# Attention, expert layer and FFN in one kernel: a conversion operation moved between an activation's maximum and its low part, two first products side by side at each group boundary, and two weight pieces converted around expert 7's third block

## The chip, the cores and the metric

The kernel runs on one core of one Trainium2 chip. The metric is the device time of one execution in microseconds (us). The engines are named as the profile names them: PE is TensorE (matmuls), PEld its weight loads, DVE is VectorE, ACT is ScalarE, POOL is GpSimd and SP is SyncE, whose queue issues most of the loads.

## The reference

Three stages follow each other; float64 weights `w_in` and `w_out` come in for the last one.

```python
def reference(**kw):
    attn_out = _attn_ref(...)                    # windowed attention with memory slots
    x = attn_out.transpose(0, 2, 1, 3).reshape(1536, 512)
    x = _moe_ref(x, w_gate, w1, w2, capacity)    # top-1 of 8 experts, 512 -> 1024 -> 512, at most 384 rows each
    return _moe2_ref(x, w_in, w_out)

def _moe2_ref(x, w_in, w_out):                   # 1536 x 512 -> 2048 -> 512
    h = x @ w_in
    g = np.maximum(0.01 * h, h)
    return (g @ w_out).astype(np.float32)
```

## The kernel before

**Precision.** Every large product is made of three matmuls: each operand is split into a high part (rounded to the matmul's format) and a low part (the rest), and high x low, high x high and low x high are summed in PSUM. The high part is a cast on ACT, the low part a subtraction on DVE.

**Experts.** `expert(e)` runs the eight experts one after the other. A branch at L762 (`self.tc.If(cnt > j * P)`) executes `block` for the third 128 rows where an expert has that many; expert 7 has. `block` transposes the gathered rows into `tp` (L858), makes `xc` (high: ACT L860, low: DVE L861), does 12 matmuls for each of two halves of the hidden layer (L874), takes the maximum in two halves of the columns (ACT L877, DVE L878 into `hh`), transposes `hh` (L883), splits it (`ht`, ACT L885 and DVE L886) and does the second product (L892). Then come the first 256 rows in six phases: `units` (L772) and `rows` (L779), whose relu parts are `hs` (ACT L824, DVE L825). In expert 7 the phases also transpose the first 1024 gathered rows of the FFN's input (`make_x`: PE L699 into the one `tp` buffer or an `acc` buffer, high ACT L701, low DVE L702).

**Pieces.** The FFN's weights are 32 float64 pieces of 128 x 512, in four quarters of eight (four of `w_in`, kind A, and four of `w_out`, kind B). A piece is loaded by SP (five `raw` buffers) and made into a float32 by bit operations in `wide_stages`: two ACT operations (L132, L133), then six DVE operations (L135, L137, L139, L141, L142, L143), then the split: ACT L121 (high) and DVE L122 (low). `feed(n)` advances this by n steps. One step issues, in this order, the split of the piece before last, the six DVE operations of the last piece, and the two ACT operations of a new one. `FEED[7]` gives expert 7 four steps, `FEED_FFN` names the units of a quarter that are followed by a step.

**FFN.** 1536 sorted rows are three groups `g` of 512; each of the four quarters `q` of the hidden layer has four column blocks `f`. A unit (q, g, f) has a first product `gemm3` (12 matmuls, L945), then `act_h`, then a second product `gemm4` (12 matmuls, L965), which runs two units behind. `act_h` is a chain that changes engine at every step:

```python
nc.scalar.copy(out=t, in_=hp)                                   # ACT L951
nc.vector.scalar_tensor_tensor(out=t, in0=hp, scalar=0.01, in1=t, op0=ALU.mult, op1=ALU.max)   # DVE L952, the maximum
nc.scalar.copy(out=gt[:, 0, :], in_=t)                          # ACT L953, high
nc.vector.tensor_tensor(out=gt[:, 1, :], in0=t, in1=gt[:, 0, :].bitcast(F32), op=ALU.subtract)  # DVE L954, low
```

The second products of a group accumulate in four PSUM tiles `acc`, of which there are four in all. `add_up` scales them and adds them into `total` and `rest` (ACT L977 in the first quarter, DVE L979 after it); the next group's first `gemm4` needs the same four tiles. In the last quarter POOL stores each finished tile (L981). Instructions of an engine run in the order in which the code issues them; waits between engines are semaphores set by the tiles' dependencies.

Of the kernel before, what the change touches and what calls it, by code (L numbers as in the profile page):

```python
# [25 lines left out]
E, F1, F2 = 8, 1024, 2048  # L26
# [6 lines left out]
NQ = 4  # L33
# [9 lines left out]
        (2, 0, 0, 3, 2, 1), (2, 0, 0, 3, 2, 1), (2, 0, 0, 1, 1, 0), (1, 1, 1, 1, 0, 0))  # L43
AHEAD = ((0, (0, 1)), (0, (2, 3)), (None, ()), (1, (0, 1)), (1, (2,)), (1, (3,)))
RETIRE = (None, ("A", 0), None, ("A", 1), ("B", 0), ("B", 1))
FEED_FFN = (0, 2, 3, 4, 6, 7, 8, 10, 11)
# [7 lines left out]
class Builder:  # L54
# [69 lines left out]
    def wide_stages(self, raw, dst, eng):  # L124
# [11 lines left out]
                                op0=ALU.is_ge, op1=ALU.mult)  # L136
        dv.tensor_scalar(out=c[1], in0=c[0], scalar1=3, scalar2=0x3FFFFFFF,  # L137
# [55 lines left out]
    def weights_gen(self):  # L193
        flying, count = [], 0

        def advance():
            for rec in list(flying):
                rec[1] += 1
                if rec[1] == 1 or rec[1] == rec[2]:
                    next(rec[0], None)  # L200
                    if rec[1] > 1:
                        flying.remove(rec)
                        self.ready.add(rec[3])

        for kind, e, i, m in self.items:
# [7 lines left out]
            if e == E:  # L213
                advance()
                st = self.wide_stages(raw, (dst[:, 0, m, :], dst[:, 1, m, :]),
                                      self.nc.vector)
                next(st)
                flying.append([st, 0, self.flight, (kind, e, i, m)])
                yield
                continue  # L220
# [14 lines left out]
        while flying:  # L235
            advance()
            yield

# [286 lines left out]
    def prologue(self):  # L525
        nc = self.nc
        with ExitStack() as ctx:
# [48 lines left out]
            NU = 2 * NI  # L576
            self.W, self.ready, self.raws, self.items = {}, set(), [], self.weight_items()
# [173 lines left out]
    def expert(self, e):  # L751
# [7 lines left out]
        if nj > 2:  # L759
            cnt, nat = self.cnts.pop(e), self.natx.pop(e, [])  # L760
            for j in range(2, nj):
                with self.tc.If(cnt > j * P):  # L762
                    self.block(e, j, nat[j - 2] if j - 2 < len(nat) else None)
# [87 lines left out]
    def block(self, e, j, nat):  # L851
        nc = self.nc
        if nat is None:
            nat = self.gather(self.tab, e * self.nj + j, self.xs)
# [6 lines left out]
        nc.vector.tensor_tensor(out=xc[:, 1], in0=tp, in1=xc[:, 0].bitcast(F32), op=ALU.subtract)  # L861
        y = self.mps.tile([P, DM], F32, name="acc", tag="acc", bufs=4)
# [62 lines left out]
    def ffn(self):  # L925
# [21 lines left out]
        def act_h(s):  # L947
            hp = hps.pop(s)
            t = self.mp.tile([P, GT], F32, name="t", tag="o", bufs=2)
            gt = gs[s] = self.mp.tile([P, 2, GT], F32R, name="gt", tag="hg", bufs=4)  # L950
            nc.scalar.copy(out=t, in_=hp)  # L951
            nc.vector.scalar_tensor_tensor(out=t, in0=hp, scalar=0.01, in1=t, op0=ALU.mult, op1=ALU.max)  # L952
            nc.scalar.copy(out=gt[:, 0, :], in_=t)  # L953
            nc.vector.tensor_tensor(out=gt[:, 1, :], in0=t, in1=gt[:, 0, :].bitcast(F32), op=ALU.subtract)  # L954
# [29 lines left out]
        steps = [(q, g, f) for q in range(NQ) for g in range(NG) for f in range(HQ)]  # L984
        for n, s in enumerate(steps):
            q, g, f = s
            gemm3(s)
            act_h(s)
            if 1 < n < len(steps) - 2:
                gemm4([steps[n - 2]])  # L990
            if q == 0 and g == 1:
                self.make_x(2, f, nat)
            self.quarter = q + 1
            self.feed(n % len(steps[::NQ]) in FEED_FFN)
        gemm4(steps[-4:-3])
        gemm4(steps[-3:-2])
        gemm4(steps[-2:])
# [61 lines left out]
```

## Time and profile before

Three timed executions took 596.17, 596.9 and 598.88 us; the median is 596.9. The profiled execution took 594.74 us.

| of the profiled execution | us | share of the span |
|---|---|---|
| its own time | 594.74 | |
| span, first to last instruction | 593.0 | |
| PE busy with matmuls | 533.7 | 90% |
| PE weight loads | 432.0 | 73% |
| DVE busy | 402.5 | 68% |
| ACT busy | 298.6 | 50% |
| POOL busy | 119.6 | 20% |

The span runs from the first to the last instruction; 1.7 us of the execution lie outside it. The shares are averages over attention (to about 110 us), routing and experts (to about 307 us) and the FFN (from there to the end), which have different limits. Matmuls are pipelined: a group of 12 shows a busy time a little longer than the distance from its start to the next group's.

### The profile page before, as it was taken

To read this page: it belongs to the slowest core of one execution; us is meant where nothing else is said; L and a number is where in the kernel's file an instruction comes from. 1 tells how busy PE (TensorE), PEld (TensorE's weight loads), DVE (VectorE), ACT (ScalarE), POOL (GpSimd) and SP (SyncE) were. 2 spreads that over 40 slices of the span, in tenths; PEclk is the share of its full clock that TensorE was granted. 3 is DMA by queue.
4 is the path that set the end of the run, shared out by engine and by line. 5 is a ranking of instruction groups with operands and counts; after the bars stand their busy time and mean duration, and the time that the engine had idled before them with its cause. 6 is when DMAs were issued, how large, how long until landed. Compare 5 with 4: busy or idle time off the path is not lost.

```text
span 593.0 us, 9379 instructions
## 1 busy us (share of the span) xinstructions
PE 533.7 (90%) x3338; PEld 432.0 (73%) x3338; DVE 402.5 (68%) x680; ACT 298.6 (50%) x520; POOL 119.6 (20%) x144
## 2 busy tenths in 40 slices
PE   7799957997997997899998999998999999999995
PEld 5566635795986975677976878877878788778884
DVE  5776776877175357672787877868888788882442
ACT  7999735846173357861544464543443444422220
POOL 7333235028320015633202000000000000000222
PEclk8999976999997999899999999999999999999999
DMA  8998959998769439975343212212113111000111
GB/s 194 199 200 197 243 192 278 389 329 195 162 202 332 135 103 329 329 230 161 108 131 120 75 68 71 72 55 88 49 59 83 35 60 37 0 1 0 72 71 71
DMA packets 66378, 84.85 MB, mean 143 GB/s; under 512 B 23168, under 2 KB 39568, under 8 KB 66320
## 3 DMA queue, kind: packets, MB, share of 16 engines
q1 hardware_dynamic: 60016, 66.46, 38.5%
q0 software_dynamic: 5296, 15.77, 8.8%
q10 hardware_dynamic: 1008, 1.84, 0.8%
q8 instruction: 38, 0.62, 0.4%
q14 instruction: 20, 0.16, 0.1%
HBM read 70.66 MB, written 13.39 MB: 142 GB/s over the span
## 4 chain that ended last, share of the span: by engine, by line
DVE 30%; PE 11%; issue 8%; ACT 7%; POOL 2%; DMA 1%; POOLq 0%; ACTq 0%; DVEq 0%
DVE t L952 4%; PE acc L965 4%; DVE gt L954 4%; ACT gt L953 4%; DVE c L139 3%; DVE c L142 3%; DVE c L135 3%; DVE ring L122 3%; PE h L945 3%; DVE c L141 2%; DVE c L137 2%; DVE total L979 2%; POOL out_dram L981 2%; DVE c L143 1%; ACT ring L225 1%
## 5 line engine op out<-in xcount | busy, mean ns | idle before, releaser
L965 PE MATMUL acc<-ring,gt 128*128 128x512 f32 x576 | 140.7, 394 | 11.0 <-DVE total L979 4.3
L945 PE MATMUL h<-x,ring 128*128 128x512 f32 x576 | 138.8, 390 | 1.1 <-ACT x L701 1.1
L965 PEld LDWEIGHTS acc<-ring,gt 128*128 128x128 f32 x576 | 108.5, 190 | 37.4 <-ACT t L951 6.8
L945 PEld LDWEIGHTS h<-x,ring 128*128 128x128 f32 x576 | 107.7, 188 | 23.7 <-ACT x L701 1.5
L953 ACT CAST gt<-t 128x512 fp32r<-128x512 f32 x48 | 29.8, 621 | 110.4 <-DVE t L952 110.4
L981 POOL DMA_INDIRECT out_dram<-total,srt x8 | 8.3, 1039 | 249.3 <-DVE total L979 248.1
L954 DVE TENSOR_TENSOR gt<-t,gt 128x512 fp32r<-128x512 f32 x48 | 33.3, 694 | 33.0 <-ACT gt L953 33.0
L951 ACT COPY t<-h 128x512 f32<-128x512 f32 x48 | 28.1, 585 | 49.8 <-PE h L945 45.7
L952 DVE SCALAR_TENSOR_TENSOR t<-h,t 128x512 f32<-128x512 f32 x48 | 32.9, 684 | 30.0 <-ACT t L951 30.0
L772 PE MATMUL h<-xsT,ring 128*128 128x256 f32 x384 | 48.8, 284 | 0.7 <-DVE ring L229 0.7
L825 DVE SCALAR_TENSOR_TENSOR hs<-h,hs 128x512 fp32r<-128x512 f32 x32 | 21.7, 687 | 39.9 <-ACT hs L824 39.9
L772 PEld LDWEIGHTS h<-xsT,ring 128*128 128x128 f32 x384 | 47.1, 191 | 1.4 <-ACT ring L225 1.1
L779 PE MATMUL acc<-ring,hs 128*128 128x512 f32 x192 | 45.6, 391 | 0.0
L229 DVE TENSOR_TENSOR ring<-raw,ring 128x1024 fp32r<-128x1024 f32 x37 | 43.2, 1219 | 2.4 <-ACT ring L225 1.9
L225 ACT CAST ring<-raw 128x1024 fp32r<-128x1024 f32 x43 | 42.6, 1057 | 0.7 <-DMA raw<-in_moe_w_dram 0.7
L779 PEld LDWEIGHTS acc<-ring,hs 128*128 128x128 f32 x192 | 35.3, 188 | 7.0
L640 POOL DMA_INDIRECT nat<-xs,tab x24 | 27.5, 1145 | 54.2 <-PE tp L735 32.8
L824 ACT ACTIVATE hs<-h 128x512 fp32r<-128x512 f32 x32 | 18.9, 606 | 24.9 <-PE acc L779 23.9
L874 PE MATMUL h<-ring,xc 128*128 128x512 f32 x72 | 21.1, 446 | 8.7 <-ACT xc L860 7.8
L229 DVE TENSOR_TENSOR ring<-more,ring 128x1024 fp32r<-128x1024 f32 x21 | 24.6, 1222 | 0.8 <-ACT ring L225 0.5
L874 PEld LDWEIGHTS h<-ring,xc 128*128 128x128 f32 x72 | 14.9, 215 | 13.1 <-ACT xc L860 8.5
L784 PE MATMUL h<-ring,xsT 128*128 128x512 f32 x72 | 21.7, 458 | 3.1 <-DMA nat<-xs,tab 1.5
(184 smaller groups left out, 823.0 us busy)
## 6 DMA issues: line engine op xcount, KB each, us to landing
raw<-in_moe_w_dram SPq DMA_DIRECT2D x43, 512.0 KB, 7.0
more<-in_moe_w_dram SPq DMA_DIRECT2D x21, 512.0 KB, 7.0
raw<-in_moe_w_in_dram SPq DMA_DIRECT2D x16, 512.0 KB, 4.1
raw<-in_moe_w_out_dram SPq DMA_DIRECT2D x16, 512.0 KB, 3.3
kn<-in_k_dram SPq DMA_DIRECT2D x16, 192.0 KB, 2.8
qn<-in_q_dram SPq DMA_DIRECT2D x16, 192.0 KB, 4.6
xs<-x POOLq DMA_DIRECT2D x16, 192.0 KB, 4.6
ys<-o SPq DMA_DIRECT2D x12, 256.0 KB, 9.3
```

The lines of the kernel that those rows point to most:

```text
L225: self.nc.scalar.copy(out=hi, in_=raw)
L229: eng.tensor_tensor(out=lo[:, j:j + n], in0=raw[:, j:j + n], in1=hi[:, j:j + n].bitcast(F32), op=ALU.subtract)
L640: self.nc.gpsimd.indirect_dma_start(out=t, out_offset=None, in_=src, in_offset=bass.IndirectOffsetOnAxis(ap=idx[:, col:col + 1], axis=0))
L772: nc.tensor.matmul(hps[f // 2][:, f % 2 * 256:f % 2 * 256 + 256], w["A", f // 4][:, wi, k, c], xs[xi][:, k, :], start=(n == 0), stop=(n == ...
L779: nc.tensor.matmul(y[j], hs[f // 2][:, hi, c:c + P], w["B", f // 4][:, wi, f % 4, :], start=(f == 0 and n == 0), stop=(f == 7 and n == 2))
L874: nc.tensor.matmul(hp[i], xc[:, xi, k, :], w[:, wi, k, :], start=(n == 0), stop=(n == 11))
L945: nc.tensor.matmul(hps[s], w[:, wi, k, c], X[g][:, xi, k, :], start=(n == 0), stop=(n == 11))
L951: nc.scalar.copy(out=t, in_=hp)
L952: nc.vector.scalar_tensor_tensor(out=t, in0=hp, scalar=0.01, in1=t, op0=ALU.mult, op1=ALU.max)
L953: nc.scalar.copy(out=gt[:, 0, :], in_=t)
L954: nc.vector.tensor_tensor(out=gt[:, 1, :], in0=t, in1=gt[:, 0, :].bitcast(F32), op=ALU.subtract)
L965: nc.tensor.matmul(acc[g][i], gt[s][:, hi, i * P:(i + 1) * P], ws[s][:, wi, s[2], :], start=(s[2] == 0 and n == 0), stop=(s[2] == HQ - 1 a ...
```

## The change

`wide_stages` yields once more, so that the first of the six DVE operations (L135 before, L136 now) can be issued alone. The new `between`, called in `act_h` ahead of the low part, issues that operation for a piece whose two ACT operations have been issued; the next step then issues only the other five. The FFN's loop goes by groups, and at a boundary the last second product of a group comes ahead of the next group's second first product. `FEED_FFN` has eight units instead of nine. In expert 7 `block_x` (the transposes and `xc`) is taken out of the branch, one conversion step follows it ahead of the branch, and one follows the block; expert 7 thus has six steps instead of four.

```diff
+BLOCK_FEED = 1
-FEED_FFN = (0, 2, 3, 4, 6, 7, 8, 10, 11)
+FEED_FFN = (1, 2, 3, 5, 7, 9, 10, 11)
@@ wide_stages
         dv.scalar_tensor_tensor(out=cf[0], in0=cf[0], scalar=MIN_HIGH * MIN_HIGH, in1=hi_f,
                                 op0=ALU.is_ge, op1=ALU.mult)
+        yield
         dv.tensor_scalar(out=c[1], in0=c[0], scalar1=3, scalar2=0x3FFFFFFF,
@@ weights_gen
                 rec[1] += 1
+                if rec[1] == 1 and not rec[4]:
+                    next(rec[0])
                 if rec[1] == 1 or rec[1] == rec[2]:
@@
+    def between(self):
+        for rec in self.flying:
+            if rec[1] == 0 and not rec[4]:
+                next(rec[0])
+                rec[4] = True
+                return
@@ expert
             for j in range(2, nj):
+                xc = None
+                if e == E - 1 and j == 2:
+                    xc = self.block_x(nat[0])
+                    self.feed(BLOCK_FEED)
                 with self.tc.If(cnt > j * P):
-                    self.block(e, j, nat[j - 2] if j - 2 < len(nat) else None)
+                    self.block(e, j, nat[j - 2] if j - 2 < len(nat) else None, xc)
+            if e == E - 1:
+                self.feed(BLOCK_FEED)
@@ act_h
             nc.scalar.copy(out=gt[:, 0, :], in_=t)
+            self.between()
             nc.vector.tensor_tensor(out=gt[:, 1, :], in0=t, in1=gt[:, 0, :].bitcast(F32), op=ALU.subtract)
@@ ffn
-            if 1 < n < len(steps) - 2:
-                gemm4([steps[n - 2]])
...
+                if f == 0 and n:
+                    gemm4(groups[n - 1][2:3])
+                    gemm4(groups[n - 1][3:])
+                if f > 1 and n + 1 < len(groups):
+                    gemm4(steps[f - 2:f - 1])
```

**DVE in the FFN, a unit with a conversion step.** Before, in the order of the program, the maximum and the low part of a unit stand together and the step's seven operations follow:

```order
L952 SCALAR_TENSOR_TENSOR t<-h,t 128x512
L954 TENSOR_TENSOR gt<-t,gt 128x512
L122 TENSOR_TENSOR ring<-c,ring 128x512
L135 SCALAR_TENSOR_TENSOR c<-c,raw 128x512
L137 TENSOR_SCALAR c<-c 128x512
L139 SCALAR_TENSOR_TENSOR c<-c 128x512
L141 TENSOR_SCALAR c<-c 128x512
L142 TENSOR_TENSOR c<-raw,c 128x512
L143 TENSOR_TENSOR c<-c 128x512
```

Now, at the same place (L974 is the maximum and L977 the low part; L136 was L135, and L139 to L145 were L137 to L143):

```order
L974 SCALAR_TENSOR_TENSOR t<-h,t 128x512
L136 SCALAR_TENSOR_TENSOR c<-c,raw 128x512
L977 TENSOR_TENSOR gt<-t,gt 128x512
L123 TENSOR_TENSOR ring<-c,ring 128x512
L139 TENSOR_SCALAR c<-c 128x512
L141 SCALAR_TENSOR_TENSOR c<-c 128x512
L143 TENSOR_SCALAR c<-c 128x512
L144 TENSOR_TENSOR c<-raw,c 128x512
L145 TENSOR_TENSOR c<-c 128x512
```

One operation has moved from the step to the place between maximum and low part; the count is the same.

**PE at a group boundary of the FFN** (from the second quarter's first group, `x_4887`, to its second, `x_5117`). Before, first and second products alternate:

```order
L945 MATMUL h<-x_4887,ring 128x512 x12
L965 MATMUL acc<-ring,gt 128x512 x12
L945 MATMUL h<-x_5117,ring 128x512 x12
L965 MATMUL acc<-ring,gt 128x512 x12
L945 MATMUL h<-x_5117,ring 128x512 x12
L965 MATMUL acc<-ring,gt 128x512 x12
L945 MATMUL h<-x_5117,ring 128x512 x12
L965 MATMUL acc<-ring,gt 128x512 x12
```

Now (L967 is the first product, L988 the second, `x_4913` and `x_5143` the same two groups):

```order
L967 MATMUL h<-x_4913,ring 128x512 x12
L988 MATMUL acc<-ring,gt 128x512 x12
L967 MATMUL h<-x_5143,ring 128x512 x12
L988 MATMUL acc<-ring,gt 128x512 x24
L967 MATMUL h<-x_5143,ring 128x512 x24
L988 MATMUL acc<-ring,gt 128x512 x12
```

The two last second products of the old group stand together, and two first products of the new group stand between them and its first second product, where there was one.

**DVE around expert 7's third block.** Before, from the copy of expert 6's output to the first `hs` of expert 7:

```order
L846 COPY o<-acc 128x512
L762 COMPARE_AND_BRANCH
L861 TENSOR_TENSOR xc<-tp,xc 128x512
L878 TENSOR_SCALAR hh<-h 128x256
L886 TENSOR_TENSOR ht<-tp,ht 128x512
L878 TENSOR_SCALAR hh<-h 128x256
L886 TENSOR_TENSOR ht<-tp,ht 128x512
L905 COPY o<-acc 128x256
L762 UNCONDITIONAL_BRANCH x2
L809 UNCONDITIONAL_BRANCH
L825 SCALAR_TENSOR_TENSOR hs<-h,hs 128x512
```

Now, from `xc` to the first `hh` of the block; the same seven conversion operations stand a second time between the block's `o` and the first `hs`:

```order
L877 TENSOR_TENSOR xc<-tp,xc 128x512
L123 TENSOR_TENSOR ring<-c,ring 128x512
L136 SCALAR_TENSOR_TENSOR c<-c,raw 128x512
L139 TENSOR_SCALAR c<-c 128x512
L141 SCALAR_TENSOR_TENSOR c<-c 128x512
L143 TENSOR_SCALAR c<-c 128x512
L144 TENSOR_TENSOR c<-raw,c 128x512
L145 TENSOR_TENSOR c<-c 128x512
L778 COMPARE_AND_BRANCH
L900 TENSOR_SCALAR hh<-h 128x256
```

Seven DVE operations now stand ahead of `hh`, and seven ahead of `hs`. The steps' ACT operations (high part of one piece, two operations of another) stand at the same places in ACT's queue. The FFN has 26 low parts of pieces (L123) where it had 28 (L122).

## Rows read from the trace of the kernel before

**Rows 1.** Busy time by stretch: us, PE, PEld, DVE, ACT, POOL, PEclk, DMA.

```profile
412.00:463.00 51.00, 46.22 (x202) 37.49 (x201) 43.83 (x72) 19.51 (x34) 0.00 (x0) 1.00 0.23 71
530.00:570.00 40.00, 40.00 (x179) 33.12 (x178) 14.94 (x23) 9.59 (x16) 4.43 (x4) 1.00 0.07 27
```

**Rows 2.** Groups by line, whole span: busy, mean ns, idle before and releasers.

```profile
L965 PE MATMUL acc<-ring,gt 128*128 128x512 f32 x576 | 140.7, 394 | 11.0 <-DVE total L979 4.3 <-DVE rest L979 2.9 <-DVE ring L122 2.8
```

**Rows 3.** Timeline of PE in the FFN: start, duration, idle before.

```profile
358.81 2.88 PE L945 MATMUL h<-x,ring 128*128 128x512 f32 x12
...
390.21 3.02 PE L965 MATMUL acc<-ring,gt 128*128 128x512 f32 x12 [0.96 <-ACT rest L977]
...
529.33 2.97 PE L965 MATMUL acc<-ring,gt 128*128 128x512 f32 x12 [1.42 <-DVE rest L979]
...
570.22 5.60 PE L945 MATMUL h<-x,ring 128*128 128x512 f32 x24
575.66 11.04 PE L965 MATMUL acc<-ring,gt 128*128 128x512 f32 x48
```

**Rows 4.** Groups by line of DVE, 412 to 530 us.

```profile
L954 DVE TENSOR_TENSOR gt<-t,gt 128x512 fp32r<-128x512 f32 x21 | 14.5, 693 | 14.4 <-ACT gt L953 14.4
```

**Rows 5.** Timeline of DVE in the FFN, a unit with a step, and `add_up`.

```profile
398.70 0.68 DVE L952 SCALAR_TENSOR_TENSOR t<-h,t 128x512 f32<-128x512 f32 x1
400.07 0.69 DVE L954 TENSOR_TENSOR gt<-t,gt 128x512 fp32r<-128x512 f32 x1 [0.69 <-ACT gt L953]
400.68 0.69 DVE L122 TENSOR_TENSOR ring<-c,ring 128x512 fp32r<-128x512 f32 x1
401.28 0.69 DVE L135 SCALAR_TENSOR_TENSOR c<-c,raw 128x512 f32<-128x512 f32 x1
402.00 0.43 DVE L137 TENSOR_SCALAR c<-c 128x512 uint32<-128x512 uint32 x1
...
404.99 0.69 DVE L952 SCALAR_TENSOR_TENSOR t<-h,t 128x512 f32<-128x512 f32 x1
...
413.25 2.72 DVE L979 SCALAR_TENSOR_TENSOR total<-acc,srt,total 128x512 f32<-128x512 f32 x4
```

**Rows 6.** Timeline of PE, the first units of the FFN.

```profile
306.66 8.46 PE L945 MATMUL h<-x,ring 128*128 128x512 f32 x36
315.35 2.99 PE L965 MATMUL acc<-ring,gt 128*128 128x512 f32 x12 [0.23 <-DVE ring L122]
318.17 2.88 PE L945 MATMUL h<-x,ring 128*128 128x512 f32 x12
323.64 4.60 PE L965 MATMUL acc<-ring,gt 128*128 128x512 f32 x12 [2.59 <-DVE ring L122]
...
353.90 2.35 PE L945 MATMUL h<-x,ring 128*128 128x512 f32 x9 [1.06 <-ACT x L701]
```

**Rows 7.** Busy time by stretch, columns as in rows 1: after the longest wait.

```profile
324.00:327.00 3.00, 3.00 (x8) 2.30 (x7) 2.83 (x6) 0.38 (x1) 0.00 (x0) 0.50 0.00 0
```

**Rows 8.** Timeline of DVE, expert 7's third block and first phase.

```profile
268.43 0.69 DVE L861 TENSOR_TENSOR xc<-tp,xc 128x512 fp32r<-128x512 f32 x1 [1.26 <-ACT xc L860]
271.69 0.42 DVE L878 TENSOR_SCALAR hh<-h 128x256 f32<-128x256 f32 x1 [2.56 <-ACT hh L877]
...
280.81 0.42 DVE L905 COPY o<-acc 128x256 f32<-128x256 f32 x1 [3.66 <-ACT o L904]
284.44 0.69 DVE L825 SCALAR_TENSOR_TENSOR hs<-h,hs 128x512 fp32r<-128x512 f32 x1 [3.21 <-ACT hs L824]
```

**Rows 9.** Timeline of PE, expert 7: transposes in the block and of the FFN's rows.

```profile
272.66 0.60 PE L883 MATMUL tp<-ident,hh 128*128 128x128 f32 x4
...
286.83 1.04 PE L699 MATMUL tp<-ident,nat 128*128 128x128 f32 x8
...
303.07 0.66 PE L699 MATMUL tp<-ident,nat 128*128 128x128 f32 x4 [0.36 <-DVE x L702]
```

**Rows 10.** Timeline of ACT, first quarter: `add_up` of the first group.

```profile
341.62 2.42 ACT L977 ACTIVATE total<-acc,srt 128x512 f32<-128x512 f32 x4
```

More of the change, by code (lines that the diff above doesn't have):

```diff
@@ L193, in weights_gen @@
     def weights_gen(self):
-        flying, count = [], 0
+        flying, count = self.flying, 0
         def advance():
@@ L217, in weights_gen @@
                 next(st)
-                flying.append([st, 0, self.flight, (kind, e, i, m)])
+                flying.append([st, 0, self.flight, (kind, e, i, m), False])
                 yield
@@ L576, in prologue @@
             NU = 2 * NI
+            self.flying = []
             self.W, self.ready, self.raws, self.items = {}, set(), [], self.weight_items()
@@ L849, in expert, with block_x @@
             (nc.scalar if e >= E - 2 else nc.sync).dma_start(out=self.ys[r0:r0 + P, :], in_=o[j])
-    def block(self, e, j, nat):
+    def block_x(self, nat):
         nc = self.nc
-        if nat is None:
-            nat = self.gather(self.tab, e * self.nj + j, self.xs)
         xc = self.mp.tile([P, 2, KD, P], F32R, name="xc", tag="hg", bufs=4)
@@ L861, in block @@
         nc.vector.tensor_tensor(out=xc[:, 1], in0=tp, in1=xc[:, 0].bitcast(F32), op=ALU.subtract)
+        return xc
+    def block(self, e, j, nat, xc):
+        nc = self.nc
+        if xc is None:
+            xc = self.block_x(self.gather(self.tab, e * self.nj + j, self.xs) if nat is None else nat)
         y = self.mps.tile([P, DM], F32, name="acc", tag="acc", bufs=4)
@@ L982, in add_up @@
                         ap=self.srt[:, t, 0:1], axis=0), in_=o, in_offset=None)
[L984 to L988, printed above, removed]
-            if 1 < n < len(steps) - 2:
-                gemm4([steps[n - 2]])
[L991 to L997, printed above, removed]
+        groups = [[(q, g, f) for f in range(HQ)] for q in range(NQ) for g in range(NG)]
+        for n, steps in enumerate(groups):
+            for f, s in enumerate(steps):
+                q, g = s[:2]
+                gemm3(s)
+                act_h(s)
+                if q == 0 and g == 1:
+                    self.make_x(2, f, nat)
+                if f == 0 and n:
[3 more added lines that the diff above has]
+                    gemm4(steps[f - 2:f - 1])
+                self.quarter = q + 1
+                self.feed(g * HQ + f in FEED_FFN)
+        gemm4(groups[-1][:1])
+        gemm4(groups[-1][1:2])
+        gemm4(groups[-1][2:])
     def build(self):
```

## The prediction

> **What bounds the kernel now.** I read the busy times by stretch first. In the FFN from 412 to 463 us PE is busy 46.22 of 51 us and DVE 43.83, while from 530 to 570 us, where no pieces are converted any more, PE is busy for all 40 us and DVE for 14.94 [rows 1]. So PE has gaps exactly where DVE also converts weights. The groups by line say what ended the gaps: the second product waited 11.0 us in all, 7.2 of them for `add_up` on DVE and 2.8 for the low part of a weight piece [rows 2]. The timeline of PE then gives the size. 24 matmuls take 570.22 to 575.66, 5.44 us, so 12 take 2.72 us when nothing holds PE. Between 358.81 and 570.22 lie 37 pairs of one first and one second product, 201.3 us at that pace, but 211.4 us go by: 10.1 us are lost to waits at the first second product of a group and to the restarts behind them. There are six such waits over 0.9 us; the first, at 390.21, and the last, at 529.33, are shown [rows 3].
>
> Why `add_up` comes late is a sum on DVE. In a unit with a step, the maximum starts at 398.70, the low part at 400.07, the step's first operation at 400.68 and the next maximum at 404.99: 1.98 us for the unit, of which DVE idles 0.69 because the low part waits for the cast on ACT, and 4.31 us for the step; four additions take 2.7 [rows 5]. A group of four units with three steps and additions costs DVE 4 x 1.98 + 3 x 4.31 + 2.7 = 23.6 us. PE needs 8 x 2.72 = 21.8. DVE is therefore 1.8 us per such group too slow, and although its busy share is below PE's, it sets the pace. The holes are regular: 21 low parts waited 14.4 us from 412 to 530 us, 0.69 each [rows 4].
>
> **The change, part by part.** *The operation between maximum and low part.* It takes 0.72 us from its start to the next operation's (401.28 to 402.00), and the hole is 0.69 [rows 5]. The low part would start 0.61 + 0.72 = 1.33 us after the maximum, and starts at 1.37 today because of ACT, so I take the operation as free and a step as 4.31 - 0.72 = 3.59. The cover is ACT's cast; without it the price is 0.72 for each of 25 pieces in the FFN. Its own inputs are two ACT operations of the step before, which stand ahead of the unit's first copy in ACT's queue, so it adds no wait. A group with three steps now costs 4 x 1.98 + 3 x 3.59 + 2.7 = 21.4, one with two 17.8, both under PE's 21.8. Behind the operation on DVE stands only the low part.
>
> *Two first products side by side.* The second product of a group's last unit comes 2.72 us earlier than it did, and the new group's first one has 5.44 us instead of 2.72 behind it. I walked one group from the start of its first product (0): second products of the old group to 8.16, two first products to 13.6, then the tiles are needed. DVE in the steady state has the old group's last low part done at 2.9 (its third matmul is due at 5.9), its last step at 6.5, the new unit at 8.5 and the additions at 11.2, the first of them at 9.2, against 13.6. The slack is about 3 us at the low part and 4 at the additions, and the second unit's maximum can't start before 11.5 in any case, so nothing piles up. With both edits the 10.1 us go to nothing; bounds are 0 and 10.1, and I take all of it because each wait has over 2 us of slack.
>
> *The first units.* The first three first products start at 306.66 and would end at 314.8; the second products start at 315.35 and, after 318.17 + 2.72 = 320.9, at 323.64, because the low parts of pieces 5 and 6 come late. The 12 matmuls after the long wait are busy for 4.60 us where others are for 2.88, at a granted clock of 0.50, the lower of the two levels [rows 6, 7]. That is 0.5 + 2.8 + 1.7 = 5.0 us. With two more steps in expert 7 both low parts are done before the FFN starts: -5.0.
>
> *Two steps around the block.* The first puts 4.31 us behind `xc`: 268.43 + 0.61 + 4.31 = 273.35 instead of 271.69 for DVE's half of `hh` [rows 8]. PE's transposes at 272.66 need it from their third matmul on, at 272.84, and get it at 273.85: 1.0 us [rows 9]. The second starts after the block's `o`, at 280.81 + 0.42 + 1.0 = 282.2, or up to 1.1 us later, since ACT issues the store of `o` and casts the high part first; I take 283.3, which ends at 287.6, and `hs`, 284.44 before, is 3.1 late [rows 8]. The low parts of the FFN's rows stand behind it, and PE's transposes at 286.83 + 1.0 need the one `tp` buffer back at 288.9: another 1.0. From `hs` on DVE has work without a gap to the end of the expert, as the wait at 303.07 for the same buffer shows, so PE, 2.0 late by then, loses the rest there and enters the FFN 3.1 us late [rows 9]. Bounds: 0 if the 10 us in which DVE is idle there hide both, 2 x 4.31 = 8.6 if they hide nothing. I take +3.1. The hoisted transposes and `xc` ran here anyway, since the block is executed.
>
> *The FFN's third group of rows* is transposed in the first quarter. There PE lost 1.06 us at 353.90 [rows 6]. Now four additions on ACT, 2.42 us [rows 10], stand ahead of the second unit's copy, because both second products come first; its low part of the rows comes later and, with one `tp` buffer, I expect 1.2 and 0.4 us of waiting in place of the 1.06: +0.5. Bounds: -1.1 and +2.4.
>
> Sum: -10.1 - 5.0 + 3.1 + 0.5 = -11.5. Of the profiled execution's 594.7 that leaves 583.2; the runs' median is 2.2 above it, so I predict 596.9 - 11.5 = 585.4 us. The loads keep their order and are five buffers ahead, and what follows PE's last matmul is unchanged.
>
> **The rivals.** *The operation is not free* (its start waits, or it slows the cast): a group with three steps stays at 23.6, 1.8 above PE; four such groups with additions on DVE are left (two in the second quarter, two in the third), at most 7.2 us, and with their slack about half: 589, at worst 592.6. For it speaks that the hole and the operation are equal to 0.03 us; against it that both lines are repeated to 0.01 us over many units.
>
> *PE is the bound, and the edits in the FFN buy nothing.* Then the 10.1 us stay in some other form and only the first units gain: 596.9 - 5.0 + 3.1 + 0.5 = 595.5. For it speaks PE's higher busy time in the stretch, 46.22 against 43.83 [rows 1]; against it that every wait is ended by DVE or ACT and that PE has none once the conversions are over. The Trainium skill, in "Perfetto Trace Analysis", section "Identifying the Most-Contended Engine", says that the engine of highest occupancy is the one to improve; by that rule it would be PE here and this rival would come true. The same page asks for a look at each regime and at bubbles that other engines cause, and there the trace disagrees with a reading by occupancy alone: the 0.69 us holes count as idle, yet DVE can't use them before the change.
>
> *The steps around the block are hidden, or not at all.* 0 instead of 3.1 gives 582.3; 8.6 gives 590.9. DVE is idle for 2.56, 3.66 and 3.21 us there [rows 8], but in separate pieces, which is why I stand between.
>
> *Slower: the clock falls.* The new waits in expert 7 and the first quarter, three or four of 0.4 to 1.4 us, stand closer together than before. If each sent the clock to its lower level as the wait of 2.59 us did, each would cost 1.7 us [rows 6, 7]; the result passes 596.9 from seven falls, or from 23 us of matmuls at half speed. Against it: from 412 to 463 us, with several of the waits at group boundaries, it stayed 1.00 [rows 1]. The Trainium skill, in "TensorE: Matmul & The Clock Gate", section "HAM oscillation — how this bites in real kernels", warns that PE which waits between bursts starts each burst at the lower clock; by that, as an estimate, the result would be some 5 us higher, about 590. The trace bears it out for the 2.59 us wait alone.
>
> **How the numbers follow.** The forecast, with its own range of 582.5 to 588, has a chance of 0.63; the operation not free 0.15; PE the bound 0.07; the steps fully hidden or fully paid 0.12; slower 0.03. The range of 581.5 to 590.5 takes in the forecast, the hidden steps and the nearer half of the first rival. About 0.5%, 3 us, is what a measurement of this kernel can tell from no change: faster than 593.9 is everything but the second and the last rival, 0.90; same 0.07; slower 0.03.
>
> **What would show it.** Right: no wait for `total`, `rest` or the low part of a piece at second products after the first quarter; the conversion operation in the hole, with the low part 1.33 to 1.40 us after the maximum; the first products starting at about 310 us; two or three waits for `x` or `tp` between 285 and 350 us. Wrong: waits of over 0.5 us at the group boundaries, a low part later than 1.5 us, a first product later than 313 us or earlier than 308 us, or a granted clock under 0.9 between 270 and 580 us.

## The result, and the profile after

| | before | after |
|---|---|---|
| median, us | 597.16 (596.17 to 598.88, 4 runs) | 582.92 (582.67 to 583.26, 4 runs) |
| profiled execution: time / span, us | 594.74 / 593.0 | 583.01 / 581.2 |
| ratio of the times, 95% interval | 1 | 0.9768 (0.9743 to 0.9792) |

The kernel is 2.3% faster; 585.4 us was predicted, with a range of 581.5 to 590.5. The two profiled executions differ by 593.0 - 581.2 = 11.8 us. The medians of the runs differ by 14.2, because the four runs of before lie 1.4 to 4.1 us above its profiled execution, while those of after lie within 0.4 of theirs.

The groups by line of the page after. The second product, which had waited 11.0 us [rows 2], waits for nothing:

```profile
L967 PE MATMUL h<-x,ring 128*128 128x512 f32 x576 | 136.5, 389 | 0.0
L988 PE MATMUL acc<-ring,gt 128*128 128x512 f32 x576 | 136.4, 390 | 0.0
```

Busy time by stretch, columns as in [rows 1]. PE is busy without a gap from 354 us to the last first products, at a granted clock of 1.00; before, it was busy 46.22 of 51 us from 412 to 463 us:

```profile
354.45:416.00 61.55, 61.55 (x273) 50.98 (x272) 47.67 (x79) 29.86 (x53) 0.00 (x0) 1.00 0.22 69
416.00:482.00 66.00, 66.00 (x293) 54.66 (x292) 56.46 (x93) 27.70 (x50) 0.00 (x0) 1.00 0.21 64
482.00:555.73 73.73, 73.73 (x327) 61.02 (x326) 48.26 (x77) 22.83 (x40) 4.74 (x5) 1.00 0.04 15
```

The timeline of DVE, one unit with a step, answers to [rows 5]. The added operation (L136) starts at 324.41 and the low part (L977) at 325.18, 1.37 us after the maximum, as it did before and now without idle time. From one maximum to the next it is 5.56 us; it was 6.29:

```profile
323.81 0.68 DVE L974 SCALAR_TENSOR_TENSOR t<-h,t 128x512 f32<-128x512 f32 x1
324.41 0.68 DVE L136 SCALAR_TENSOR_TENSOR c<-c,raw 128x512 f32<-128x512 f32 x1
325.18 0.69 DVE L977 TENSOR_TENSOR gt<-t,gt 128x512 fp32r<-128x512 f32 x1
325.79 0.69 DVE L123 TENSOR_TENSOR ring<-c,ring 128x512 fp32r<-128x512 f32 x1
...
329.37 0.68 DVE L974 SCALAR_TENSOR_TENSOR t<-h,t 128x512 f32<-128x512 f32 x1
```

The timeline of PE, expert 7 and the FFN, answers to [rows 3, 6, 9]; the block's first product before the change stands ahead of it:

```profile
268.18 4.65 PE L874 MATMUL h<-ring,xc 128*128 128x512 f32 x19 [1.57 <-ACT xc L860]
```

```profile
268.24 4.61 PE L896 MATMUL h<-ring,xc 128*128 128x512 f32 x19 [1.50 <-ACT xc L876]
...
273.88 0.44 PE L905 MATMUL tp<-ident,hh 128*128 128x128 f32 x2 [0.81 <-DVE hh L900]
...
289.15 1.09 PE L711 MATMUL tp<-ident,nat 128*128 128x128 f32 x8 [1.11 <-DVE x L714]
...
306.59 0.66 PE L711 MATMUL tp<-ident,nat 128*128 128x128 f32 x4 [1.48 <-DVE x L714]
...
310.20 8.44 PE L967 MATMUL h<-x,ring 128*128 128x512 f32 x36
...
342.32 0.66 PE L711 MATMUL tp<-ident,nat 128*128 128x128 f32 x4 [0.95 <-DVE x L714]
...
563.89 11.04 PE L988 MATMUL acc<-ring,gt 128*128 128x512 f32 x48
```

Here the difference can be split in two. The block's first product begins at 268.2 in both kernels. From there to the first product of the FFN it was 306.66 - 268.2 = 38.5 us and is 310.20 - 268.2 = 42.0: the block steps cost 3.5. From there to PE's last matmul it was 575.66 + 11.04 - 306.66 = 280.0 and is 563.89 + 11.04 - 310.20 = 264.7: the FFN gives 15.3. 3.5 - 15.3 = -11.8.

### The profile page after: what moved, and what is told of

Its sections match the earlier page's. It is cut to its first block, busy times and chain, and to the rows that moved or that the text cites. A ratio compares the mean times of both kernels' runs of the same rounds, so it can differ in the third digit from the quotient of the medians.

```text
span 581.2 us, 9375 instructions
## 1 busy us (share of the span) xinstructions
PE 530.0 (91%) x3338; PEld 431.3 (74%) x3338; DVE 401.7 (69%) x680; ACT 297.7 (51%) x520; POOL 118.6 (20%) x144
## 4 chain that ended last, share of the span: by engine, by line
PE 35%; DVE 8%; issue 7%; ACT 3%; POOL 2%; DMA 1%; ACTq 0%; POOLq 0%
PE acc L988 16%; PE h L967 15%; POOL out_dram L1004 2%; DVE c L141 1%; DVE c L144 1%; PE acc L811 1%; DVE ring L123 1%; PE acc L914 1%; DVE t L974 1%; DVE x L714 1%; DVE c L143 1%; ACT gt L975 1%; DMA ys<-o 1%; DVE c L139 1%; DVE c L145 1%
## 5 line engine op out<-in xcount | busy, mean ns | idle before, releaser
L967 PE MATMUL h<-x,ring 128*128 128x512 f32 x576 | 136.5, 389 | 0.0
L988 PE MATMUL acc<-ring,gt 128*128 128x512 f32 x576 | 136.4, 390 | 0.0
L967 PEld LDWEIGHTS h<-x,ring 128*128 128x128 f32 x576 | 108.0, 188 | 22.4
L988 PEld LDWEIGHTS acc<-ring,gt 128*128 128x128 f32 x576 | 107.9, 188 | 22.3
L974 DVE SCALAR_TENSOR_TENSOR t<-h,t 128x512 f32<-128x512 f32 x48 | 33.0, 687 | 39.8 <-ACT t L973 39.8
L843 DVE SCALAR_TENSOR_TENSOR hs<-h,hs 128x512 fp32r<-128x512 f32 x32 | 21.8, 688 | 38.4 <-ACT hs L842 38.4
L977 DVE TENSOR_TENSOR gt<-t,gt 128x512 fp32r<-128x512 f32 x48 | 33.3, 693 | 18.0 <-ACT gt L975 15.8
L652 POOL DMA_INDIRECT nat<-xs,tab x24 | 25.3, 1053 | 57.2 <-PE tp L747 34.0
L896 PE MATMUL h<-ring,xc 128*128 128x512 f32 x72 | 22.5, 469 | 7.8 <-ACT xc L876 7.7
L122 ACT CAST ring<-c 128x512 fp32r<-128x512 f32 x32 | 19.8, 618 | 10.6 <-DVE c L145 9.6
```

What stands on the lines that cost most here:

```text
L652: self.nc.gpsimd.indirect_dma_start(out=t, out_offset=None, in_=src, in_offset=bass.IndirectOffsetOnAxis(ap=idx[:, col:col + 1], axis=0))
L896: nc.tensor.matmul(hp[i], xc[:, xi, k, :], w[:, wi, k, :], start=(n == 0), stop=(n == 11))
L967: nc.tensor.matmul(hps[s], w[:, wi, k, c], X[g][:, xi, k, :], start=(n == 0), stop=(n == 11))
L988: nc.tensor.matmul(acc[g][i], gt[s][:, hi, i * P:(i + 1) * P], ws[s][:, wi, s[2], :], start=(s[2] == 0 and n == 0), stop=(s[2] == HQ - 1 a ...
```

## The experiments

The parts were taken out one at a time and put into the kernel before one at a time. Each is read by the same two lengths, since the moment at which a program comes to expert 7's block differs by up to 2.4 us between single executions (267.2 to 269.6) before any edit acts. "Block steps" means the two steps in expert 7 together with the list of eight steps a quarter that goes with them; without them the list has nine (no_block and the two split kernels apart, as said there). Each ratio is to before as it was timed in the same set of runs; its median was 597.16 us in the set of after, 595.82 in that of only_fill, only_order, old_order and no_fill, and 596.93 in that of the other four, so up to 1.3 us between medians of different sets is not the kernels'.

| kernel | operation | order | block steps | block to FFN | FFN | median, us (lowest to highest) | ratio to before (95%) |
|---|---|---|---|---|---|---|---|
| before | - | - | - | 38.5 | 280.0 | 597.16 | 1 |
| only_fill | x | - | - | 38.5 | 268.2 | 583.03 (580.1 to 583.7) | 0.9773 (0.9739 to 0.9808) |
| only_order | - | x | - | 38.5 | 279.6 | 594.11 (592.2 to 596.1) | 0.9967 (0.994 to 0.9993) |
| only_block | - | - | x | 42.0 | 268.7 | 589.39 (587.9 to 590.9) | 0.9876 (0.9834 to 0.9919) |
| no_block | x | x | - | 38.4 | 271.6 | 586.98 (585.3 to 587.7) | 0.9822 (0.9781 to 0.9862) |
| old_order | x | - | x | 41.9 | 263.6 | 582.74 (581.5 to 583.3) | 0.9786 (0.9764 to 0.9808) |
| no_fill | - | x | x | 41.9 | 268.7 | 586.22 (585.9 to 586.9) | 0.9846 (0.9824 to 0.9868) |
| after | x | x | x | 42.0 | 264.7 | 582.92 (582.7 to 583.3) | 0.9768 (0.9743 to 0.9792) |
| split_step | x | x | one, cut | 38.4 | 264.7 | 581.42 (579.9 to 583.3) | 0.9737 (0.9705 to 0.9769) |
| split_old | x | - | one, cut | 38.4 | 263.6 | 578.92 (577.5 to 586.0) | 0.9714 (0.9668 to 0.9761) |

**no_fill**: the changed kernel without the operation in the hole.

```diff
             nc.scalar.copy(out=gt[:, 0, :], in_=t)
-            self.between()
             nc.vector.tensor_tensor(out=gt[:, 1, :], in0=t, in1=gt[:, 0, :].bitcast(F32), op=ALU.subtract)
```

> The changed kernel with the conversion operation back behind the low part, ahead of the step's other five; the rest of the change stays. Theory (DVE's sum per group sets the pace where it is above PE's 21.8 us): a group with three steps and additions costs DVE 23.6 us again, there are four of them, so PE waits 3 to 7 us in all at the group boundaries of the second and third quarter, and the time is 586 to 590 us. Rival (the order of the products, or the two pieces moved to expert 7, made the gain): no waits there, 583 us.

586.22 us, and the waits are elsewhere. The timeline of PE has one of 0.28 at a group boundary (468.51), and three at the transposes of the third group's rows in the first quarter:

```profile
338.81 0.66 PE L711 MATMUL tp<-ident,nat 128*128 128x128 f32 x4 [1.61 <-DVE x L714]
343.48 0.66 PE L711 MATMUL tp<-ident,nat 128*128 128x128 f32 x4 [1.28 <-DVE x L714]
350.37 0.66 PE L711 MATMUL tp<-ident,nat 128*128 128x128 f32 x4 [0.74 <-DVE x L714]
...
468.51 3.29 PE L987 MATMUL acc<-ring,gt 128*128 128x512 f32 x12 [0.28 <-ACT gt L975]
```

The FFN is 4.0 us longer than in the changed kernel (268.7 against 264.7). So the price of the operation was near what was expected, but not by the place: with the new order a group of 23.6 us on DVE passes its boundary almost without a wait.

**old_order**: the changed kernel with the order of products of before.

```diff
-                if q == 0 and g == 1:
-                    self.make_x(2, f, nat)
-                if f == 0 and n:
-                    gemm4(groups[n - 1][2:3])
-                    gemm4(groups[n - 1][3:])
-                if f > 1 and n + 1 < len(groups):
-                    gemm4(steps[f - 2:f - 1])
...
+            if 1 < n < len(steps) - 2:
+                gemm4([steps[n - 2]])
+            if q == 0 and g == 1:
+                self.make_x(2, f, nat)
```

The edit that the table calls "order" holds a second move, which the diff under "The change" leaves out: the transposes of the third group's rows (`make_x`) stand ahead of the unit's second product, where they stood behind it.

> The changed kernel with the order of first and second products of before; the rest of the change stays. Theory (DVE's sum decides; the order only adds slack): DVE has the additions done 2 us before the tiles are due in this order too, so no waits over 0.3 us at the group boundaries, 582 to 584 us. Rival (the room of a second first product is what removed the waits): waits of 1 to 2 us at six or more boundaries, 590 us or more.

582.74 us, not to be told from the changed kernel by the runs. PE has no wait at all in the FFN; its length of 263.6 us is 1.1 below the changed kernel's, which has the wait of 0.95 at 342.32, at those transposes. The order buys nothing once the operation is there; which of its two moves costs the 1.1 us was not run apart.

**only_fill**: the kernel before with the operation alone (the new `yield`, `between` and its call).

> The kernel before with the conversion operation between maximum and low part, nothing else: nine steps per quarter, the old order, four steps in expert 7. Theory: a group with three steps costs DVE 21.4 us, under PE's 21.8, so the 10 us of waits at the boundaries go and the 5 us in the first units stay: span 9 to 11 us shorter than before, 585 to 588 us. Rival (both edits are needed): half of it or less, 591 us or more.

583.03 us, lower than expected: the operation alone brings as much as the whole change. All waits at the boundaries are gone, as expected. What is left, on PE's timeline, is the opening, and there less than the 5.0 us of before:

```profile
316.06 2.97 PE L977 MATMUL acc<-ring,gt 128*128 128x512 f32 x12 [0.39 <-DVE ring L122]
...
323.62 4.42 PE L977 MATMUL acc<-ring,gt 128*128 128x512 f32 x12 [1.87 <-DVE ring L122]
```

0.4 + 1.9 + (4.42 - 2.88 = 1.5) = 3.8 us. With the block steps and the list of eight (old_order) the FFN is 4.6 us shorter, 263.6 against 268.2, and starts 3.5 later. These buy little more than they cost.

**only_order**: the kernel before with the new order alone.

> The kernel before with the new order of the products, nothing else. Theory: DVE's 23.6 us per group stay above PE's 21.8, so PE waits as long as before, at the boundaries or at the last second product of a group, which is now due 2.7 us earlier: within 2 us of before, 595 to 599 us. Rival (the order removes the waits): 588 us or less.

594.11 us, just under before (595.82 in the same set). The timeline of PE shows why it is not more: one wait over 0.5 us is left at a boundary, and three of about 2.5 stand in the first quarter where there was one:

```profile
324.01 4.59 PE L965 MATMUL acc<-ring,gt 128*128 128x512 f32 x12 [2.58 <-DVE ring L122]
...
337.17 4.60 PE L965 MATMUL acc<-ring,gt 128*128 128x512 f32 x12 [2.65 <-DVE ring L122]
...
350.13 0.66 PE L699 MATMUL tp<-ident,nat 128*128 128x128 f32 x4 [2.41 <-DVE x L702]
350.55 4.59 PE L965 MATMUL acc<-ring,gt 128*128 128x512 f32 x12
...
446.26 3.31 PE L965 MATMUL acc<-ring,gt 128*128 128x512 f32 x12 [0.85 <-ACT gt L953]
```

DVE has the same work as before, and the FFN takes the same 280 us, though not by the same losses. Busy time by stretch, columns as in [rows 1], first before, then only_order:

```profile
306.80:576.00 269.20, 257.16 (x1123) 209.32 (x1123) 200.69 (x325) 109.52 (x193) 12.11 (x12) 0.99 0.19 58
```

```profile
306.80:576.00 269.20, 260.19 (x1126) 212.12 (x1125) 201.22 (x325) 108.72 (x193) 11.78 (x12) 0.98 0.19 59
```

PE waited 12.0 us there and waits 9.0. But 12 matmuls take 4.59 or 4.60 us behind three waits where they did behind one, 1.7 us more each time, and two more such stretches give the 3 us back. The order moved the waits to the front; what it took off them went into matmuls at a lower granted clock.

That suggested a theory which the prediction does not have: what counts is not whether each group is even by itself, but DVE's sum, holes included, over the three quarters that convert, against PE's 36 units of 5.44 = 195.8 us. Four kernels, of the second set of runs, went after the block steps and the place of their cost.

**no_block**: the changed kernel with `BLOCK_FEED = 0` in place of 1 (the list keeps eight steps a quarter).

> The changed kernel without its two block steps (the filler operation, the new order of products and the new list of steps stay). Theory: the block steps buy the opening of the FFN. Without them the first products start at about 307 us (310.20 with them), and second products of the first group wait for the low parts of late pieces, two waits of about 2.1 and 3.3 us, one of them followed by matmuls at the lower clock (+1.7): 585 to 588 us. Rival: only_fill, without block steps, paid only 2.3 us of waits and 1.6 of clock there, so the steps cost as much as they buy: 582 to 584 us. Second rival: the pieces come in time without them, and the kernel gains the 3.4 us of the later start: 579 to 580 us.

586.98 us, as the theory had it. The opening waits for the low parts are longer than in only_fill, as PE's timeline shows:

```profile
318.53 3.00 PE L988 MATMUL acc<-ring,gt 128*128 128x512 f32 x12 [2.43 <-DVE ring L123]
...
335.92 4.42 PE L988 MATMUL acc<-ring,gt 128*128 128x512 f32 x12 [2.77 <-DVE ring L123]
```

The first of them goes with a list whose steps begin one unit later than in only_fill. The second stands at the fourth second product, which the new order puts one first product earlier; only_order waits there too, 2.65 us at 337.17, with the list of nine.

**only_block**: the kernel before with the block steps and the list of eight alone (old_order without the line `self.between()`).

> The kernel before with the two block steps and the new list of steps (eight a quarter), without the filler operation and with the old order of products. Theory: the waits at the group boundaries are cured twice over, by the shorter VectorE sum of a step or by the later second products, and either is enough; with neither, groups with three steps need 23.6 us of VectorE against 21.8 of TensorE, and waits of 1 to 1.9 us for total and rest come back at five or six boundaries, 6 to 9 us in sum. Opening as in the changed kernel (start at about 310 us, no wait). 589 to 593 us. Rival: the shorter list of steps (eight a quarter in place of nine) is what freed the boundaries in no_fill: no waits there, 582 to 586 us.

589.39 us, in the range of the theory, but by fewer boundaries than it said: two waits for `total` (0.78 and 1.44) rather than five or six, and one each for the transposes and for `x`. Eight steps a quarter had freed most of the boundaries by themselves. The timeline of PE, all its waits from 315 us on:

```profile
340.82 0.66 PE L711 MATMUL tp<-ident,nat 128*128 128x128 f32 x4 [1.54 <-DVE x L714]
...
354.22 2.35 PE L967 MATMUL h<-x,ring 128*128 128x512 f32 x9 [0.21 <-ACT x L713]
...
411.75 3.02 PE L987 MATMUL acc<-ring,gt 128*128 128x512 f32 x12 [0.78 <-DVE total L1001]
...
478.92 2.98 PE L987 MATMUL acc<-ring,gt 128*128 128x512 f32 x12 [1.44 <-DVE total L1001]
```

no_fill has the same DVE work in the other order and the same FFN, 268.7 us: its waits stand in the first quarter, these at the boundaries too. (Its median is lower, but the two were timed in different sets and their ratios overlap; in its profiled execution the block began 2.1 us earlier.) In this pair the order moves the waits and keeps their sum, 3.9 and 4.0 us, at a granted clock of 1.00 in both FFNs.

**split_step**: one step, cut in two, in place of the two block steps. The first three DVE operations of the next piece stay ahead of the branch, the other three wait behind the block; the first quarter has nine steps.

```diff
                                op0=ALU.bitwise_and, op1=ALU.bitwise_or)
+        yield
         dv.tensor_scalar(out=c[0], in0=c[1], scalar1=0xFF800000, scalar2=None, op0=ALU.bitwise_and)
...
+                    self.holding = True
                     self.feed(BLOCK_FEED)
+                    self.holding = False
...
             if e == E - 1:
-                self.feed(BLOCK_FEED)
+                for st in self.held:
+                    next(st)
...
-                self.feed(g * HQ + f in FEED_FFN)
+                self.feed(g * HQ + f in (FEED_FFN if q else FEED_FIRST))
...
+FEED_FIRST = (0, 1, 3, 5, 7, 8, 9, 10, 11)
```

> In place of two whole block steps one step is cut in two: its high and low part and the first half of another piece's VectorE operations ahead of the branch, the other half behind it; the first quarter has nine steps again. Filler and new order stay. Theory: the 3.1 to 3.4 us by which the block steps delay TensorE in expert 7 come from VectorE's 4.3 us in one piece ahead of the xs subtraction and of the transposes; cut in two, TensorE enters the FFN at 306.8 to 308 us, without waits at the opening: 579 to 581 us. Rival: one piece fewer is ready at the opening, a wait of about 2 us with a stretch at the lower clock returns, and nothing is won: 582 to 584 us.

581.42 us in the median, its profiled execution 580.82. From the block to the FFN it takes 38.4 us, what it took before the change, and the opening has no wait. So half a step at each of the two places costs nothing, where a whole step at each costs 3.5 us together, and one step fewer is enough for the opening. The run changes the number of steps and the cut at once; whether one whole step at one of the places would be free too was not run.

**split_old**: the same with the old order of products.

> As split_step, with the old order of products. Theory: with the filler operation the order buys nothing at the boundaries, and in the first quarter it costs the wait of 0.95 us for x; so 0.5 to 1.5 us faster than split_step: 578 to 580 us. Rival: the order matters once the start is earlier: boundary waits for total or rest return, 581 to 584 us.

578.92 us (five of its six runs 577.5 to 579.5), the lowest median here. PE's answer on its waits from 255 us to the end of the FFN has three lines, and in the FFN itself PE waits nowhere:

```profile
PE h L906 <- ACT xc L886: 1.5, 1, 1.5
PE tp L718 <- DVE x L721: 0.3, 1, 0.3
PE acc L821 <- ACT hs L852: 0.3, 1, 0.3
```

Its span is 576.7, 4.5 us below the changed kernel's: 3.5 from the block, 1.1 from the first quarter.

**more_1, more_2, more_3** test the sum by itself. In the changed kernel one DVE operation of each step in the FFN (0.43 us) is done two, three or four times; it gives the same values again.

```diff
-        dv.tensor_scalar(out=c[1], in0=c[0], scalar1=3, scalar2=0x3FFFFFFF,
-                         op0=ALU.logical_shift_left, op1=ALU.bitwise_and)
+        for _ in range(2 if self.quarter else 1):
+            dv.tensor_scalar(out=c[1], in0=c[0], scalar1=3, scalar2=0x3FFFFFFF,
+                             op0=ALU.logical_shift_left, op1=ALU.bitwise_and)
```

> The changed kernel with one VectorE operation of each conversion step in the FFN done twice (the shift and mask into c, 0.43 us, which gives the same values again). Theory: what counts is VectorE's sum over the three quarters that convert, against 36 units of TensorE at 5.44 us = 195.8: 36 units of 1.98, 26 steps of 3.59 and two quarters' additions of 8.1 make 180.8 now; 26 times 0.43 more makes 192.0, still below. So no waits at the products and at most 1 us more at the first quarter's transposes: 583 to 584.5 us. Rival: each group must be even by itself; one with three steps has 21.4 + 1.3 = 22.7 against 21.8, and loses 0.9 us six times over: 587 to 589 us.

> As more_1, with that operation done three times. Theory of the sum: 180.8 + 26 x 0.85 = 203.0, 7.2 over TensorE's 195.8: 588 to 592 us, with the waits in the first quarter or at the groups, wherever the order puts them. Rival (groups): 24.0 against 21.8 in a group with three steps, 2.2 us six times over, 13 us: 595 to 597 us.

> As more_1, with that operation done four times. Theory of the sum: 180.8 + 26 x 1.28 = 214.1, 18.3 over: 598 to 604 us, 11 us above more_2. Rival (groups): 25.2 against 21.8, 3.4 us six times over, 21 us, and groups with two steps even at 20.4: 603 to 606 us.

585.23, 591.29 and 601.10 us. Ratios to before, 594.99 us in this set, are 0.983 (0.9797 to 0.9864), 0.9943 (0.9923 to 0.9963) and 1.0092 (1.0059 to 1.0125); the profiled spans are 1.2, 8.2 and 18.1 us above the changed kernel's 581.2. more_2 and more_3 came out in the ranges of the sum and below what the rule by groups gives; more_1 fell between the two, 0.7 above the sum's range. It has no wait at any boundary, so the rule by groups is wrong there too; its loss is at the first quarter's transposes. Its timeline of PE:

```profile
338.39 0.66 PE L712 MATMUL tp<-ident,nat 128*128 128x128 f32 x4 [0.76 <-DVE x L715]
343.05 0.66 PE L712 MATMUL tp<-ident,nat 128*128 128x128 f32 x4 [1.23 <-DVE x L715]
349.68 0.66 PE L712 MATMUL tp<-ident,nat 128*128 128x128 f32 x4 [0.51 <-DVE x L715]
```

The sum itself has to be set right, though. 26 low parts of pieces are done in the FFN, but between the first maximum and the 37th, which is 36 units, lie only 24 steps and five additions, beside four low parts of rows. In the kernels without waits at the opening, the trace gives DVE's time over these 36 units and the part of it in which DVE waited (the holes ahead of low parts count as work). The last column is the FFN's length less the shortest, 263.6.

| kernel | 36 units on DVE, us | of it waits | work and holes, less 195.8 | FFN less 263.6 |
|---|---|---|---|---|
| old_order | 193.4 | 19.2 | -21.6 | 0 |
| after | 194.7 | 20.3 | -21.4 | 1.1 |
| more_1 | 197.7 | 13.2 | -11.3 | 2.8 |
| only_block | 200.5 | 9.7 | -5.0 | 5.1 |
| no_fill | 200.9 | 10.2 | -5.1 | 5.1 |
| more_2 | 206.1 | 10.7 | -0.3 | 9.1 |
| more_3 | 216.2 | 9.7 | 10.8 | 18.8 |

So the work in more_3 is 206.6 us, where 214.1 was expected, and more_2 loses 9.1 us although its work is no more than PE's. That the sum as it was put on record came near the lengths is in part luck: what it counts too much stands in for the time that DVE waits itself. In more_3 that is three waits, all early, for ACT's copy of the next first product:

```profile
344.19 0.69 DVE L975 SCALAR_TENSOR_TENSOR t<-h,t 128x512 f32<-128x512 f32 x1 [1.99 <-ACT t L974]
...
369.49 0.69 DVE L975 SCALAR_TENSOR_TENSOR t<-h,t 128x512 f32<-128x512 f32 x1 [5.56 <-ACT t L974]
...
394.50 0.69 DVE L975 SCALAR_TENSOR_TENSOR t<-h,t 128x512 f32<-128x512 f32 x1 [2.10 <-ACT t L974]
```

From 394.50 to the 37th maximum at 532.72 DVE waits for nothing but the holes, and neither does it in no_fill and more_2 from the same place on: there DVE sets the pace. In the changed kernel it still waits 8.5 us over those units. What is shown is the step from more_2 to more_3: 11.1 us more of DVE's work made the FFN 9.7 us longer. The time that DVE waits early, while it is ahead, is not made up later.

## Why the prediction was right, point by point

*The sum.* -11.5 was predicted and -11.8 measured between the profiled executions. Two of the four terms were off, by 0.4 and by 0.6 the other way; that they nearly cancel is luck, but both are small. The step that was off most is the last one, the anchor: the sum had given 583.2 of the profiled execution's 594.7, and the median of the runs came out at 582.92. Adding back the 2.2 us by which before's median lay above its own profile assumed that the changed kernel scatters as before does, and these four runs scatter less. That distance is also one of a single set: in the three sets run later before's median is 594.99 to 596.93.

*The group boundaries (-10.1).* Right in place and size: no wait is left from 354 us on. The reason given, DVE's sum per group with holes counted as work, holds in the main: taking 0.72 us out of each step removes the waits (only_fill). "With both edits the 10.1 us go to nothing" credits the order as well, and that is what the runs took back. Alone it gains 0.3% (0.1 to 0.6) by the runs and 0.4 us of the FFN's length; beside the operation the FFN is 1.1 us longer with it (after and old_order, and the two split kernels), and with eight steps a quarter and no operation it changes nothing in the FFN's length. That the shorter list also frees most of them (only_block) was not seen, so the 10.1 us have two cures in this change, and the operation is the one that works alone. And the condition is looser than the prediction put it: a group with three steps may exceed PE's 21.8 us, as in no_fill, if the groups with two give it back before a tile is missed.

*The first units (-5.0).* Right for the change made; no wait is left at the opening. But the price of leaving the steps out depends on what else is done: the FFN is 4.6 us longer beside the operation alone (only_fill against old_order), and 6.9 with the operation, the new order and the shorter list (no_block's 271.6 against 264.7).

*The two block steps (+3.1).* 3.5 measured, at the three places named: 0.81 at the transposes of `hh`, 1.11 at 289.15 and 1.48 at 306.59, where 1.0, 1.0 and the rest were expected and 0.36 stood before. By their starts [rows 9] PE is 1.0, 2.3 and 3.5 us late at the three. `hs` starts at 287.82, 3.4 late (3.1 expected). The FFN starts at 310.20.

*The third group's rows (+0.5).* One wait of 0.95 came in place of the 1.06, not 1.2 and 0.4. The term was about 0.6 too large, and its reason was incomplete: it goes by the additions on ACT and does not count that the transposes themselves moved ahead of the second product.

*The rivals.* The operation is free: the low part starts 1.37 us after the maximum, as before. The rival's case without that gain was run as no_fill: it put the loss at 589 - 585.4 = 3.6 us, and the FFN is 4.0 us longer, though the waits stand at the first quarter's transposes and not at the boundaries. PE as the bound fell: no edit gave PE less work, and the FFN lost 15.3 us. The prediction's reading by occupancy took PE's matmul time; the Trainium skill, "Perfetto Trace Analysis", section "Identifying the Most-Contended Engine", says that this is not a good measure of how close PE is to its limit and asks, beside the count of its arithmetic, for the share of its weight loads instead. Over the whole span the weight loads still name PE (73% against DVE's 68%), but from 412 to 463 us they name DVE, 43.83 us against 37.49 [rows 1], and the edit that mattered filled DVE's holes. Clock falls, the mechanism of the slower rival, did not come in the changed kernel: the granted clock is 1.00 in every stretch read from 264 to 555 us.

*What stays open.* Why before's runs scatter by some 6 us (594.2 to 600.5 in the 13 runs of one set) and the four of after by 0.6 was not tried. Waits at many boundaries, whose length moves with small shifts, would do it, but that is only argued; and split_old, which has none, shows one run at 585.98 among its six.

## What to carry to other kernels

Count an in-order engine's holes as its work, and compare its sum with that of the engine it feeds over the stretch in which it does not wait itself; slack from earlier, while it is ahead, does not help there. In two pairs of kernels here, in which the feeding engine was short of time, a new order of the consumer left the length as it was; where the feeding engine had time to spare, the order bought nothing. The cheapest time to win is an operation that is ready anyway, put into a hole of the same length. When two or three edits cure one wait, run each alone before keeping all: here one operation did what the whole change did, and of the work put around the branch half as much, in two shorter pieces, served the opening as well and cost nothing there.

## What was not expected of the hardware

The length of a wait alone did not tell whether the granted clock falls behind it. After 1.87 us, before's boundary at 414.14 went on at 1.00 (12 matmuls in 2.98 us), and only_fill's second product at 323.62 at 0.65 (4.42 us). In no_block 2.43 us were followed by 1.00 and 2.77 by 0.68; in only_order 12 matmuls behind a wait of 2.41 us took 4.59. 1.00 is the upper of the clock's two levels; 0.65 and 0.68 are means over stretches that lie in part at the lower, 0.50. First before's boundary:

```profile
414.14 2.98 PE L965 MATMUL acc<-ring,gt 128*128 128x512 f32 x12 [1.87 <-DVE total L979]
```

Busy time by stretch, columns as in [rows 1], of before behind that wait, of only_fill, and of no_block, where the second line is the one that fell:

```profile
414.20:417.00 2.80, 2.80 (x13) 2.31 (x14) 2.37 (x4) 0.40 (x1) 0.00 (x0) 1.00 0.00 0
```

```profile
324.00:327.00 3.00, 3.00 (x11) 2.35 (x10) 2.90 (x5) 0.36 (x1) 0.00 (x0) 0.65 0.08 12
```

```profile
318.60:321.40 2.80, 2.80 (x13) 2.29 (x14) 2.66 (x5) 0.57 (x2) 0.95 (x2) 1.00 0.58 170
336.20:339.00 2.80, 2.80 (x10) 2.19 (x10) 2.50 (x4) 1.38 (x2) 0.00 (x0) 0.68 0.00 0
```

In only_fill an earlier wait of 0.39 stands 7.6 us ahead of the one that fell; what else differs between these places, the runs do not show.
